# Seven half-size products in the second MLP stage of the first chunk of an attention and MLP kernel

## Chip, cores and metric

The kernel runs on one core of one Trainium2 chip. The metric is the device time of one execution in microseconds (us), the median over runs. All times of instructions come from one profiled execution and are counted from the start of its span.

## What is computed

Linear attention over 8 batches, 8 heads, 576 tokens and head size 64, and behind it a layer norm and an MLP with a residual, in float32 at the edges:

```python
q_s = softmax(q, axis=-1)                      # over the head's 64 numbers
k_s = softmax(k, axis=2)                       # over the tokens
kv = einsum('bhsd,bhse->bhde', k_s, v)
x  = einsum('bhsd,bhde->bhse', q_s, kv)        # heads put side by side: 8 x 576 x 512
xn = (x - mean(x)) / sqrt(var(x) + 1e-06) * g_ln
out = x + maximum(xn @ w_ch1, 0.0) @ w_ch2     # 512 -> 2048 -> 512
```

## The kernel before

**Tiling.** A chunk is 512 tokens of one batch, as four token tiles of 128. Chunks 0 to 7 are the first 512 tokens of batches 0 to 7, and a ninth chunk holds the last 64 tokens of all eight. Work runs chunk by chunk. A chunk has a first MLP stage (16 row tiles of 128 hidden units, from 512 inputs, then relu into hT) and a second stage (16 row tiles of hT as the contraction, 512 output columns). The weights stay in SBUF in bf16: w1_sb (raw), w1g (scaled by g_ln), w2_sb.

**Products.** From chunk 1 on, both stages use a scheme of seven block products in place of eight (for 2 x 2 blocks). It needs sums of blocks ahead of the products: sum_h (line 576) builds four sums of hT blocks on VectorE, quarter_w2 (line 563) four of w2 in w2_q, sum_x (line 255) four of the normed input on GpSimd, and sum_w1 (line 242) four of w1 in the columns of w1_sb whose raw values are no longer needed. Some results are then passed between PSUM banks by a ScalarE copy (copy_u, line 628, and the seeds) and a VectorE add (add_u, line 632). sum_w1 has two parts: part 1 serves the upper eight row tiles, which chunk 1 uses, and part 0 the lower eight, which chunk 2 uses first. In chunk 0 all of the second stage is plain: mm2_stream (line 552) makes 64 matmuls of 512 columns, 16 for each of four token tiles, each tile in its own PSUM bank, and y_out (line 533) takes a bank out by one VectorE instruction of 512 columns and a store.

**Order of the work.** The order on every engine is written out by hand. run (line 849) walks over the matmul steps of a chunk, each with a weight (1 is a matmul of 512 columns, 0.5 one of 256), and issues a side step as soon as the sum of the weights reaches the position given with it. Engines, and the DMA queues of GpSimd and SyncE, then execute what they were given in this order; an instruction that waits holds all behind it on its engine. In chunk 0 the first stage has positions 0 to 64 and the second 64 to 128. Lines 1109 to 1141 are chunk 0's side steps, second_side (line 896) is chunk 1's. Chunk 0's side steps include the preparation of chunk 1: exp_qt and reduce_q (softmax of q), eq_pT (four transposes on TensorE and a ScalarE copy), exp_k and prep_kvrem (exponentials of k), cast_v (copies of v to vm), kv_pairs (line 357: 40 small matmuls, then a reciprocal and two multiplications on VectorE into kv_sb), po_x (line 1104: four matmuls that need kv_sb, then x_fast on VectorE), xn_pT (transposes of the normed chunk).

**Loads.** load_behind (line 1067) puts loads for batches 1 and 2 into the GpSimd queue at the start; its load_krem is the load of the last 64 tokens of k (tile ktr, two DMAs of 64 KB), which prep_kvrem reads. load_batch (line 1077) puts later loads of q and k into the SyncE queue.

Of the kernel before, what the change touches and what calls it, by code (L numbers as in the profile page):

```python
# [12 lines left out]
FP32 = mybir.dt.float32  # L13
BF16 = mybir.dt.bfloat16
AF = mybir.ActivationFunctionType
ALU = mybir.AluOpType
# [4 lines left out]
def kernel(  # L21
# [21 lines left out]
    P = 128  # L43
# [183 lines left out]
    def reduce_q(c, t, tn=1):  # L227
        ts = slice(t, t + tn)
        nc.vector.reduce_sum(eqs[c][1][:, ts], eqs[c][0][:, ts], axis=AX.X)  # L229
# [9 lines left out]
        at = DH // 2 * (1 - part)  # L239
        return w1_sb[:, n, at : at + DH // 2].rearrange("p (ko i n) -> p ko i n", ko=2, n=P)  # L240

    def sum_w1(i, part):

        ps = slice(4 * part, 4 * part + 4)
        blocks = w1g.rearrange("p (kh ko) (i odd n) -> p kh ko i odd n", kh=2, odd=2, n=P)
        a11, a12, a21, a22 = [blocks[:, kh, :, ps, odd, :] for odd in range(2) for kh in range(2)]
        s1, s2, s3, s4 = [w1_sum(n, part) for n in range(4)]
        dst, x, y, op = (
            (s1, a21, a22, ALU.add), (s2, s1, a11, ALU.subtract),
            (s4, a12, s2, ALU.subtract), (s3, a11, a21, ALU.subtract),  # L250
        )[i]
        for ko in range(2):
            nc.vector.tensor_tensor(out=dst[:, ko], in0=x[:, ko], in1=y[:, ko], op=op)

    def sum_x(c, i, ts=range(2)):

# [273 lines left out]
            else:  # L530
                nc.scalar.activation(dst, ph, AF.Relu)

    def y_out(c, t, pc, cols=slice(0, 512), eng=None):
        if cols.start == 0:
            hbox["ot"] = outp.tile([P, DM], FP32, tag="ot", name="ot")
        ot = hbox["ot"][:, cols]
        nc.vector.scalar_tensor_tensor(
            ot, in0=pc, scalar=rstds[c][:, t : t + 1], in1=xs[c][0][:, t, cols],
            op0=ALU.mult, op1=ALU.add,
        )  # L540
        eng = eng or nc.gpsimd
        if c < B:
            eng.dma_start(
                out[c, 0:SM, :].rearrange("(p t) n -> p t n", t=T)[:, t, cols], ot
            )
        else:
            for half in range(2):
                eng.dma_start(
                    out[2 * t + half, SM:S, cols], ot[64 * half : 64 * half + 64]
                )  # L550

    def mm2_stream(c, t, ko):

        if ko == 0:
            hbox["pc", t] = mm_ps.tile([P, DM], FP32, tag="m", name="pc")
        nc.tensor.matmul(  # L556
            hbox["pc", t], hbox["h"][:, ko, t, :], w2_sb[:, ko, :],
            start=(ko == 0), stop=(ko == KO2 - 1),
        )
        if ko == KO2 - 1:  # L560
            y_out(c, t, hbox["pc", t], eng=nc.sync if t > 1 else nc.gpsimd)

    def quarter_w2(i, k0, kn):

        ks = slice(k0, k0 + kn)
# [20 lines left out]
        )[i]  # L586
        nc.vector.tensor_tensor(out=dst, in0=x, in1=y, op=op)  # L587

    def prod(n, bank, t, k, first=False, own=False, c0=0, cn=DH2):

        at = slice(t * P, t * P + P)
        cs = slice(c0, c0 + cn)
        if n in (1, 2, 4):
            odd, half = ((0, 0), (1, 0), None, (1, 1))[n - 1]
            lhsT = hbox["h"][:, 2 * k + odd, 2 * half + t, :]
        else:
            lhsT = hbox["s"][:, {5: 0, 6: 1, 7: 2, 3: 3}[n], k, at]
# [6 lines left out]
        nc.tensor.matmul(hbox[bank][:, t, cs], lhsT, rhs[:, cs],  # L604
                         start=first and (own or t == 0) and k == 0,
                         stop=k == KH - 1, skip_group_check=True)
# [4 lines left out]
    def y_quarter(c, t, col, src):  # L611
        if (c, t) not in ybox:
            ybox[c, t] = outp.tile([P, DM], FP32, tag="ot", name="ot")
            ynum[c, t] = 0
        cols = slice(DH2 * col, DH2 * col + DH2)
        nc.vector.scalar_tensor_tensor(
            ybox[c, t][:, cols], in0=src, scalar=rstds[c][:, t : t + 1],
            in1=xs[c][0][:, t, cols], op0=ALU.mult, op1=ALU.add,
        )
        ynum[c, t] += 1  # L620
        if ynum[c, t] == 2:
            nc.gpsimd.dma_start(
                out[c, 0:SM, :].rearrange("(p t) n -> p t n", t=T)[:, t], ybox[c, t]
            )

# [5 lines left out]

    def add_u(dst, src):
        nc.vector.tensor_tensor(out=hbox[dst], in0=hbox["b"], in1=hbox[src], op=ALU.add)

    def last_products(product):

# [183 lines left out]
    def mlp_steps(c):  # L820
        if c > FAST:
            return mm1_fast(c) + mm2_fast(c)
        first = []
        if c == 0:
            first = [
                (0.5, lambda m=m, ko=ko: mm1_part(c, m, 0, 2, ko))
                for kh in range(2) for m in range(4) for ko in (2 * kh, 2 * kh + 1)
            ]
            parts = ((0, 2, 1), (1, 0, 2), (0, 3, 1), (2, 0, 2), (1, 2, 2), (2, 2, 2), (3, 0, 2), (3, 2, 2))
        else:  # L830
            parts = ((0, 0, 2), (1, 0, 2), (0, 2, 2), (1, 2, 2))
        for n, t0, tn in parts:
            first += [
                (0.25 * tn, lambda m=m, t0=t0, tn=tn, ko=ko: mm1_part(c, m, t0, tn, ko))
                for m in range(4 * n, 4 * n + 4) for ko in range(KO1)
            ]
        if c == 0:
            return first + [
                (1, lambda t=t, ko=ko: mm2_stream(c, t, ko))
                for k0, kn in ((0, 4), (4, 4), (8, 4), (12, 2), (14, 2))  # L840
                for t in range(T) for ko in range(k0, k0 + kn)
            ]
        return first + mm1_fast(c, (2,)) + mm2_fast(c)

    def spread(fns, a, b):
# [50 lines left out]
    def second_side():  # L896
# [6 lines left out]
        s += [(p, lambda j=j: cast_v(2, j)) for j, p in enumerate((23, 32.2))]  # L903
        s += [(at, lambda i=i: sum_x(1, i)) for i, at in enumerate((9.1, 9.2, 31.5, 36))]
        s += [(66, lambda: load_v(3, True))]
        s += [(9 + 2 * t, lambda t=t: reduce_q(2, t, 2)) for t in (0, 2)]
        s += [(36, lambda: recip_q(2))]
        s += [(18, lambda: exp_k(2, 0, 4)), (28.5, lambda: exp_k(2, 2, 4)), (33, lambda: prep_kvrem(2))]
# [158 lines left out]
    def load_behind(b, parts=(2, 0, 1)):  # L1067

        alloc(b, parts)
        for which in parts:  # L1070
            if which == 1:
                load_v(b)
                load_krem(nc.gpsimd, b)
            else:
                load_main(nc.gpsimd, b, which, 0, H)

    def load_batch(b, parts=(2, 0), after=None):

        alloc(b, parts)
        for which in parts:  # L1080
            if after is None:
                nc.vector.memset(raws[b][which][0:1, 0, 0, 0:1], 0.0)
            else:
                nc.gpsimd.tensor_copy(out=raws[b][which][0:1, 0, 0, 0:4], in_=after)
        for which in parts:
            hn = H // 2 if (b, which) == (B - 1, 2) else H
            for h0 in range(0, H, hn):
                load_main(nc.sync, b, which, h0, hn)
        if 0 in parts:
            load_krem(nc.sync, b)  # L1090

    with tc.manual_schedule(
# [2 lines left out]
    ):  # L1095
        first_batch()
        load_behind(1, (2, 0))
        load_w2(2)
        load_behind(1, (1,))
        load_w2(3, 0, 2)  # L1100
        load_w2(3, 2, 2)
        load_behind(2)

        def po_x(c, t):
            for i in range(NP):
# [34 lines left out]
            + [(p, lambda t=t: xn_pT(1, t, nc.scalar)) for t, p in enumerate((119, 122.5, 127.9))]  # L1140
            + [(p + 0.1, lambda t=t: square_sum(1, t)) for t, p in enumerate((119, 122.5))]

        )
        for c in range(1, B):
# [46 lines left out]
```

## Time and profile before

| | |
|---|---|
| median of 3 runs | 262.92 us (262.43 to 263.71) |
| the profiled execution's own time | 262.68 us |
| its span | 260.9 us |
| TensorE (PE) busy, granted clock | 254.9 us (98%), 0.997 |
| VectorE (DVE), ScalarE (ACT), GpSimd (POOL) busy | 223.3, 177.8, 103.4 us |
| chunk 0, first stage | about 15.2 to 31.3 us |
| chunk 0, second stage | 31.3 to 48.6 us |
| chunk 1 | 48.6 to 76.2 us |

The span runs from the first to the last instruction; 1.78 us of the execution's own time lie outside it. A line of the timeline gives the start, the time from the first start to the last end of the merged instructions, engine, source line, operation, tiles, shapes and count, and in brackets how long the engine was idle before it and what ended that. Since an instruction's end overlaps the start of the next on its engine, the step from one start to the next is shorter than a duration.

### The profile page before, as it was taken

Reading aid. Unit: us, or ns where it says so; the run is one execution under the profiler, and the core shown is the slowest. Engines: PE = TensorE matmul, PEld = TensorE weight load, DVE = VectorE, ACT = ScalarE, POOL = GpSimd, SP = SyncE. Lnnn points to the kernel's source line nnn. Section 1 sums busy time; section 2 is a strip of 40 time slices with the busy share of each in tenths; the row PEclk is TensorE's granted clock in tenths of the full one; section 3 lists DMA queues with packets and bytes.
Section 4 is the critical chain, followed back from the end, with each engine's and each line's share of the span. In section 5 each row is a group of like instructions: output and inputs, shape, how many; then the busy total and the mean of one; then the engine's idle time right before and its main releaser. Section 6 shows DMA issues by size and latency. Waiting matters only on the chain.

```text
span 260.9 us, 7328 instructions
## 1 busy us (share of the span) xinstructions
PE 254.9 (98%) x2904; PEld 218.6 (84%) x2907; DVE 223.3 (86%) x542; ACT 177.8 (68%) x348; POOL 103.4 (40%) x160
## 2 busy tenths in 40 slices
PE   8999999999999999999999999999999999999993
PEld 5889855788888888888888888888888888888883
DVE  6778996989998998899889988998899889957873
ACT  4657790997987785788578857885788386638400
POOL 3953138230199409800890098009100910190000
PEclk9999999999999999999999999999999999999998
DMA  6999999998899996998889968998902630322014
GB/s 190 255 206 206 352 221 274 275 213 273 151 121 314 272 110 139 293 242 88 119 287 259 95 133 290 244 96 166 276 1 45 140 143 4 72 72 101 3 40 121
DMA packets 82618, 45.04 MB, mean 173 GB/s; under 512 B 58196, under 2 KB 79192, under 8 KB 82584
## 3 DMA queue, kind: packets, MB, share of 16 engines
q0 software_dynamic: 32464, 21.76, 44.9%
q1 hardware_dynamic: 49488, 22.29, 37.0%
q10 hardware_dynamic: 632, 0.53, 0.7%
q8 instruction: 22, 0.36, 0.6%
q14 instruction: 12, 0.10, 0.1%
HBM read 36.70 MB, written 9.44 MB: 177 GB/s over the span
## 4 chain that ended last, share of the span: by engine, by line
PE 92%; DMA 4%; POOL 2%; issue 0%; DVE 0%
PE ba L604 21%; PE bx L762 20%; PE bb L762 10%; PE ph L520 8%; PE bb L604 6%; PE be L604 5%; PE bc L604 5%; PE pc L556 5%; PE bc L762 5%; DMA w_raw<-in_moe_w_ch_dram 3%; PE pkv L371 2%; DMA qt<-in_q_dram 2%; PE po L403 2%; PE ptr L928 1%; PE po L414 1%; POOL v L1006 1%
## 5 line engine op out<-in xcount | busy, mean ns | idle before, releaser
L604 PEld LDWEIGHTS <-hs 128*128 128x128 bf16 x512 | 49.6, 98 | 6.0
L269 POOL TENSOR_TENSOR tq<-xnT 128x256 bf16<-128x256 bf16 x30 | 20.1, 671 | 85.5 <-PE bc L604 59.9
L762 PEld LDWEIGHTS <-w_raw 128*128 128x128 bf16 x480 | 46.6, 98 | 5.8 <-DVE bb L793 0.2
L604 PEld LDWEIGHTS <-hT 128*128 128x128 bf16 x392 | 37.6, 98 | 4.2
L762 PEld LDWEIGHTS <-w1g 128*128 128x128 bf16 x360 | 34.7, 98 | 4.3 <-issue 0.2
L762 PE MATMUL bx<-tq,w_raw 128*128 128x256 bf16 x240 | 31.5, 273 | 0.0
L604 PE MATMUL ba<-w_q,hs 128*128 128x256 bf16 x256 | 30.6, 273 | 0.0
L786 ACT COPY bc<-bx 128x512 f32<-128x512 f32 x30 | 16.7, 594 | 19.1 <-PE bx L762 19.1
L427 ACT ACTIVATE scrap<-x,mv 128x512 bf16<-128x512 bf16 x32 | 23.1, 723 | 4.6 <-DVE mv L457 4.4
L793 DVE TENSOR_TENSOR bb<-bx,s 128x512 f32<-128x512 f32 x30 | 19.5, 694 | 7.8 <-ACT s L790 5.1
L804 ACT ACTIVATE hT<-bb 128x512 bf16<-128x512 f32 x30 | 16.3, 594 | 9.5 <-PE bb L762 9.5
L804 ACT ACTIVATE hT<-bc 128x512 bf16<-128x512 f32 x30 | 16.4, 595 | 8.5 <-PE bc L762 8.5
L796 DVE TENSOR_TENSOR hT<-bx,s 128x512 bf16<-128x512 f32 x30 | 19.3, 684 | 2.9 <-PE bx L762 2.7
L587 DVE TENSOR_TENSOR hs<-hT 128x1024 bf16<-128x1024 bf16 x32 | 21.3, 672 | 0.5 <-ACT hT L804 0.5
L229 DVE TENSOR_REDUCE zq<-eq 128x16 f32<-128x1024 bf16 (+1 forms) x20 | 20.7, 1048 | 0.5 <-ACT eq L220 0.5
L269 POOL TENSOR_TENSOR tq<-xnT,tq 128x256 bf16<-128x256 bf16 x30 | 20.0, 669 | 1.1
L449 DVE SCALAR_TENSOR_TENSOR x<-po,rq 128x256 bf16<-128x256 f32 x48 | 17.5, 420 | 1.6 <-PE po L403 1.6
L790 ACT COPY s<-bb 128x512 f32<-128x512 f32 x30 | 16.5, 620 | 0.0
L804 ACT ACTIVATE hT<-bx 128x512 bf16<-128x512 f32 x30 | 16.4, 608 | 0.0
L762 PE MATMUL bx<-xnT,w1g 128*128 128x256 bf16 x120 | 16.2, 273 | 0.0
L762 PE MATMUL bx<-tq,w1g 128*128 128x256 bf16 x120 | 15.9, 272 | 0.0
L762 PE MATMUL bc<-xnT,w1g 128*128 128x256 bf16 x120 | 15.8, 273 | 0.0
(157 smaller groups left out, 539.3 us busy)
## 6 DMA issues: line engine op xcount, KB each, us to landing
out_dram<-ot POOLq DMA_DIRECT2D x30, 256.0 KB, 5.0
kt<-in_k_dram SPq DMA_DIRECT2D x5, 1024.0 KB, 12.5
qt<-in_q_dram SPq DMA_DIRECT2D x4, 1024.0 KB, 8.7
qt<-in_q_dram POOLq DMA_DIRECT2D x2, 1024.0 KB, 12.9
kt<-in_k_dram POOLq DMA_DIRECT2D x2, 1024.0 KB, 14.7
vm<-in_v_dram POOLq DMA_DIRECT2D x16, 128.0 KB, 12.5
qt<-in_q_dram SPq DMA_DIRECT2D x3, 512.0 KB, 7.2
w_raw<-in_moe_w_ch_dram POOLq DMA_DIRECT2D x3, 512.0 KB, 10.8
```

The costliest lines, as they stand in the source:

```text
L229: nc.vector.reduce_sum(eqs[c][1][:, ts], eqs[c][0][:, ts], axis=AX.X)
L269: nc.gpsimd.tensor_tensor(out=dst[:, t], in0=x[:, t], in1=y[:, t], op=ALU.subtract)
L427: nc.scalar.activation(scrap, x[:, t], AF.Square, bias=mv[:, t, 0:1], scale=-float(DM), accum_out=mv[:, t, 1:2],)
L449: nc.vector.scalar_tensor_tensor(x[:, t].rearrange("p (i two d) -> p i two d", two=2, d=D)[:, :, half], in0=pobox[c, t][half], scalar=1.0, ...
L520: nc.tensor.matmul(ph[:, m % 2, at : at + tn], (w1g if c else w1_sb)[:, ko, m * P : (m + 1) * P], xnTs[c][:, t0 : t0 + tn, ko, :], start=( ...
L587: nc.vector.tensor_tensor(out=dst, in0=x, in1=y, op=op)
L604: nc.tensor.matmul(hbox[bank][:, t, cs], lhsT, rhs[:, cs], start=first and (own or t == 0) and k == 0, stop=k == KH - 1, skip_group_check= ...
L762: nc.tensor.matmul(dst[:, q], lhsT, rhs, start=first and q == 0 and ko == 0, stop=ko == 1, skip_group_check=True)
L786: nc.scalar.copy(at[g, "c"], at[g, "x"])
L793: nc.vector.tensor_tensor(out=at[g, "b"], in0=at[g, "x"], in1=at[g, "s"], op=ALU.add)
L796: nc.vector.tensor_tensor(out=h_out(g, 1, 1), in0=at[g, "x"], in1=at[g, "s"], op=ALU.add)
L804: nc.scalar.activation(h_out(g, odd, half), at[g, name], AF.Relu)
```

## The change

Chunk 0's second stage is split by the contraction. For hT's row tiles 0 to 7 (paired even and odd, four pairs) seven products of eight matmuls with 256 columns replace 32 matmuls with 512. Row tiles 8 to 15 stay plain, as 64 matmuls of 256 columns that add into the same four banks. The second stage has 60 units of weight after, in place of 64, and the side steps at its end are placed four units lower. The four sums of hT (sum_h0) go on VectorE into four buffers of the output pool, at positions 44 to 52. There sum_w1 for part 1 stood; it moves to positions 81 to 89. sum_w1 for part 0, which stood at 66 to 84, moves to GpSimd in chunk 1, at positions 40 to 55. Results leave by y_quarter in eight pieces of 256 columns. The last tokens of k for batch 1 are loaded from SyncE's queue at position 26 and no longer from GpSimd's. SyncE's loads of k for batch 4, and of q and k for batches 5 to 7, are each issued in two halves.

```diff
-    def sum_w1(i, part):
+    def sum_w1(i, part, eng=nc.vector):
...
-            nc.vector.tensor_tensor(out=dst[:, ko], in0=x[:, ko], in1=y[:, ko], op=op)
+            eng.tensor_tensor(out=dst[:, ko], in0=x[:, ko], in1=y[:, ko], op=op)
...
+    def sum_h0(i):
+        if i == 0:
+            hbox["s0"] = [
+                outp.tile([P, KH // 2, 2 * P], BF16, tag="ot", name="s0") for _ in range(4)
+            ]
...
+        dst, x, y, op = (
+            (s1, a21, a22, ALU.add), (s2, s1, a11, ALU.subtract),
+            (s3, a11, a21, ALU.subtract), (s4, a12, s2, ALU.subtract),
+        )[i]
+        nc.vector.tensor_tensor(out=dst, in0=x, in1=y, op=op)
...
-            nc.gpsimd.dma_start(
+            (nc.sync if c == 0 and t > 1 else nc.gpsimd).dma_start(
                 out[c, 0:SM, :].rearrange("(p t) n -> p t n", t=T)[:, t], ybox[c, t]
             )
...
+    def mm2_first():
...
+        product(1, "a", True, {7: [seed_c]})
+        product(5, "b", True)
+        product(6, "a", False, {7: [lambda: copy_u("s2")]})
+        product(2, "c", False, {1: [seed_e]})
+        product(7, "a", False, {7: [lambda: copy_u("s3")]})
+        product(3, "e", False, {1: [lambda: add_u("b", "s3")]})
+        product(4, "a")
+        for k0, kn in ((8, 4), (12, 2), (14, 2)):
+            for name, half, col in (("c", 0, 0), ("e", 0, 1), ("b", 1, 1), ("a", 1, 0)):
+                rest(name, half, col, k0, kn)
+        return steps
...
-            return first + [
-                (1, lambda t=t, ko=ko: mm2_stream(c, t, ko))
-                for k0, kn in ((0, 4), (4, 4), (8, 4), (12, 2), (14, 2))
-                for t in range(T) for ko in range(k0, k0 + kn)
-            ]
+            return first + mm2_first()
...
+        s += [(40 + 5 * i, lambda i=i: sum_w1(i, 0, nc.gpsimd)) for i in range(4)]
...
-                load_krem(nc.gpsimd, b)
+                if b > 1:
+                    load_krem(nc.gpsimd, b)
...
-            hn = H // 2 if (b, which) == (B - 1, 2) else H
+            hn = H // 2 if b > 4 or (b, which) == (4, 0) else H
...
+        nc.vector.memset(raws[1][3][0:1, 0, 0:1], 0.0)
...
+        def krem_first():
+            nc.vector.memset(raws[1][3][0:1, 0, 0:1], 0.0)
+            load_krem(nc.sync, 1)
...
-            + [(62 + t, lambda t=t: exp_qt(1, t)) for t in range(T)]
-            + [(67 + t, lambda t=t: reduce_q(1, t)) for t in range(T)]
-            + [((75, 79, 86, 90)[t], lambda t=t: eq_pT(1, t, nc.scalar)) for t in range(T)]
-            + [(78, lambda: nc.vector.reciprocal(eqs[1][2], eqs[1][1]))]
-            + [(82, lambda: exp_k(1, 0, 4)), (88, lambda: exp_k(1, 2, 4))]
+            + [((68.6, 69.6, 77.1, 78.1)[t], lambda t=t: exp_qt(1, t)) for t in range(T)]
+            + [((78, 79, 84.6, 86)[t], lambda t=t: reduce_q(1, t)) for t in range(T)]
+            + [((76, 79.5, 86, 90)[t], lambda t=t: eq_pT(1, t, nc.scalar)) for t in range(T)]
+            + [(92, lambda: nc.vector.reciprocal(eqs[1][2], eqs[1][1]))]
+            + [(86.5, lambda: exp_k(1, 0, 4)), (90.5, lambda: exp_k(1, 2, 4))]
...
-            + [(p, lambda i=i: quarter_w2(i, 0, 4)) for i, p in enumerate((58, 60, 61, 62))]
-            + [(98.5 + 0.4 * j, lambda j=j: cast_v(1, j)) for j in range(2)]
-            + [(p, lambda i=i: sum_w1(i % 4, 1 - i // 4)) for i, p in enumerate((42, 45, 50, 53, 66, 70, 80, 84))]
-            + [(99 + i, lambda i=i: quarter_w2(i, 4, 2)) for i in range(4)]
-            + [(100.4, lambda: prep_kvrem(1))]
-            + [(110, lambda: (kv_pairs(1), start_x(1)))]
-            + [(p, lambda t=t: po_x(1, t)) for t, p in enumerate((114.8, 116.5, 118.6, 121))]
+            + [(p, lambda i=i: sum_h0(i)) for i, p in enumerate((44, 46, 49.5, 52))]
+            + [(p, lambda i=i: quarter_w2(i, 0, 4)) for i, p in enumerate((56, 57, 58, 59))]
+            + [(p, lambda i=i: sum_w1(i, 1)) for i, p in enumerate((81, 83, 87, 89))]
+            + [(26, krem_first)]
+            + [(p, lambda j=j: cast_v(1, j)) for j, p in enumerate((94.5, 98.5))]
+            + [(98.6 + i / 10, lambda i=i: quarter_w2(i, 4, 2)) for i in range(4)]
+            + [(92, lambda: prep_kvrem(1))]
+            + [(106, lambda: (kv_pairs(1), start_x(1)))]
+            + [(p, lambda t=t: po_x(1, t)) for t, p in enumerate((110.8, 112.5, 114.6, 117))]
```

rest(name, half, col, k0, kn) adds the matmuls of row tiles k0 to k0 + kn - 1 for two token tiles and 256 columns into a bank, and behind the last of them calls y_quarter. seed_c copies bank a into bank c on ScalarE; seed_e adds bank b and s2 into bank e on VectorE.

More of the change, by code (lines that the diff above doesn't have):

```diff
@@ L531, in mm1_part @@
                 nc.scalar.activation(dst, ph, AF.Relu)
[L533 to L561, printed above, removed]
     def quarter_w2(i, k0, kn):
@@ L587, in sum_h, with h_sum, prod @@
         nc.vector.tensor_tensor(out=dst, in0=x, in1=y, op=op)
-    def prod(n, bank, t, k, first=False, own=False, c0=0, cn=DH2):
+    def sum_h0(i):
[3 more added lines that the diff above has]
+            ]
+        s1, s2, s3, s4 = hbox["s0"]
+        a11, a12, a21, a22 = [
+            h_part(odd, half, slice(0, KH // 2)) for half in range(2) for odd in range(2)
+        ]
+        dst, x, y, op = (
[3 more added lines that the diff above has]
+        nc.vector.tensor_tensor(out=dst, in0=x, in1=y, op=op)
+    def h_sum(n, k, at, c):
+        i = {5: 0, 6: 1, 7: 2, 3: 3}[n]
+        return hbox["s0"][i][:, k, at] if c == 0 else hbox["s"][:, i, k, at]
+    def prod(n, bank, t, k, first=False, own=False, c0=0, cn=DH2, c=None):
         at = slice(t * P, t * P + P)
@@ L596, in prod @@
         else:
-            lhsT = hbox["s"][:, {5: 0, 6: 1, 7: 2, 3: 3}[n], k, at]
+            lhsT = h_sum(n, k, at, c)
         if n in (1, 2):
@@ L633, in add_u, with product, go, rest @@
         nc.vector.tensor_tensor(out=hbox[dst], in0=hbox["b"], in1=hbox[src], op=ALU.add)
+    def mm2_first():
+        steps = []
+        def product(n, name, first=False, at=None):
+            for i in range(KH):
+                t, k = divmod(i, KH // 2)
+                def go(t=t, k=k, i=i):
+                    if first and i == 0:
+                        bank(name)
+                    prod(n, name, t, k, first, c=0)
+                    for fn in (at or {}).get(i, []):
+                        fn()
+                steps.append((0.5, go))
+        def rest(name, half, col, k0, kn):
+            for t in range(2):
+                for ko in range(k0, k0 + kn):
+                    def go(t=t, ko=ko):
+                        nc.tensor.matmul(
+                            hbox[name][:, t], hbox["h"][:, ko, 2 * half + t, :],
+                            w2_sb[:, ko, DH2 * col : DH2 * col + DH2],
+                            start=False, stop=ko == KO2 - 1, skip_group_check=True,
+                        )
+                        if ko == KO2 - 1:
+                            y_quarter(0, 2 * half + t, col, hbox[name][:, t])
+                    steps.append((0.5, go))
+        def seed_c():
+            bank("c")
+            nc.scalar.copy(hbox["c"], hbox["a"])
+        def seed_e():
+            bank("e")
+            add_u("e", "s2")
+        product(1, "a", True, {7: [seed_c]})
[9 more added lines that the diff above has]
+        return steps
     def last_products(product):
@@ L1140 @@
-            + [(p, lambda t=t: xn_pT(1, t, nc.scalar)) for t, p in enumerate((119, 122.5, 127.9))]
-            + [(p + 0.1, lambda t=t: square_sum(1, t)) for t, p in enumerate((119, 122.5))]
+            + [((68.6, 69.6, 77.1, 78.1)[t], lambda t=t: exp_qt(1, t)) for t in range(T)]
+            + [((78, 79, 84.6, 86)[t], lambda t=t: reduce_q(1, t)) for t in range(T)]
+            + [((76, 79.5, 86, 90)[t], lambda t=t: eq_pT(1, t, nc.scalar)) for t in range(T)]
+            + [(92, lambda: nc.vector.reciprocal(eqs[1][2], eqs[1][1]))]
@@ L1143 @@
+            + [(98.6 + i / 10, lambda i=i: quarter_w2(i, 4, 2)) for i in range(4)]
+            + [(92, lambda: prep_kvrem(1))]
+            + [(106, lambda: (kv_pairs(1), start_x(1)))]
+            + [(p, lambda t=t: po_x(1, t)) for t, p in enumerate((110.8, 112.5, 114.6, 117))]
+            + [(p, lambda t=t: xn_pT(1, t, nc.scalar)) for t, p in enumerate((115, 118.5, 123.9))]
+            + [(p + 0.1, lambda t=t: square_sum(1, t)) for t, p in enumerate((115, 118.5))]
         )
```

## The prediction

> **What bounds the kernel.** First the page's busy times, then the chain of waits, then TensorE's timeline.
>
> ```profile
> PE 254.9 (98%) x2904; PEld 218.6 (84%) x2907; DVE 223.3 (86%) x542; ACT 177.8 (68%) x348; POOL 103.4 (40%) x160
> PE   8999999999999999999999999999999999999993
> ```
>
> TensorE is busy from the second slice to the last but one, and the chain gives it 92%. So time falls only where TensorE has less to do, and rises where it is made to wait. The stage that changes:
>
> ```profile
> 34.99 1.67 PE L556 MATMUL pc<-w_sb,hT 128*128 128x512 bf16 x7
> 36.50 0.39 PE L928 MATMUL ptr<-ident,eq 128*128 128x128 bf16 x4
> 43.21 1.03 PE L556 MATMUL pc<-w_sb,hT 128*128 128x512 bf16 x4 [0.16 <-issue]
> 44.22 0.38 PE L414 MATMUL po<-kv_sb,eqT 128*128 128x128 bf16 x4
> ...
> 65.60 1.91 PE L604 MATMUL bb<-w_q,hs 128*128 128x256 bf16 x16
> 67.35 1.91 PE L604 MATMUL ba<-w_q,hs 128*128 128x256 bf16 x16
> ```
>
> A matmul of 512 columns takes (36.50 - 34.99) / 7 = 0.2155 us, one of 256 takes (67.35 - 65.60) / 16 = 0.1091. The stage lasts from 31.31 to 48.63. Its 64 matmuls are 13.79 us, seven transpose groups 7 x 0.22, four po groups 4 x 0.22, kv_pairs 0.76: 16.97, and so only 0.35 is waiting. VectorE is the second engine, and its end of this stage is what po waits for:
>
> ```profile
> 33.45 0.75 DVE L253 TENSOR_TENSOR w_raw<-w1g 128x512 bf16<-128x512 bf16 x2
> 34.12 2.46 DVE L229 TENSOR_REDUCE zq<-eq 128x8 f32<-128x512 bf16 x4
> ...
> 41.30 0.87 DVE L570 TENSOR_TENSOR w_q<-w_sb,w_q 128x512 bf16<-128x512 bf16 x2
> 43.09 0.18 DVE L377 RECIPROCAL rzk<-pkv 128x4 f32<-128x4 f32 x1 [0.92 <-PE pkv L371]
> 43.31 0.86 DVE L379 TENSOR_TENSOR kv_sb<-pkv,rzk 64x256 bf16<-64x256 f32 x2
> 44.64 0.69 DVE L464 SCALAR_TENSOR_TENSOR x<-po,rq 128x512 bf16<-128x512 f32 x1 [0.47 <-PE po L414]
> ```
>
> VectorE had 0.92 us to spare ahead of rzk; kv_sb is ready at 43.31 + 0.86 = 44.17, and po starts at 44.22.
>
> **TensorE's own work.** 64 x 0.2155 = 13.79 becomes 56 x 0.1091 + 64 x 0.1091 = 13.09: 0.70 less. The loads of weights double, but a load takes 98 ns and lies under 109 ns, as in every later chunk.
>
> **Bank a is handed on three times.** Products 1, 6, 7 and 4 all write it, and between two of them lie eight matmuls, 0.87 us, where later chunks have sixteen. A ScalarE copy must fit in.
>
> ```profile
> 65.80 0.57 ACT L714 COPY bc<-ba 128x512 f32<-128x512 f32 x1 [0.16 <-PE ba L604]
> ```
>
> It starts 0.20 behind the issue of the last matmul (65.60) and takes 0.57; with 0.05 to get back that is 0.82 of 0.87. Where ScalarE is free it costs nothing: seed_c runs from 32.38 to 32.95, the next product wants the bank at 33.06. For s2, two exp_qt (0.53 each) are over just as product 6 ends, and two transpose groups widen the gap: nothing. For s3, ScalarE is at eq_pT's copy until 36.64: the copy ends at 37.23, bank a was wanted at 37.20: 0.09. The three copies (0.48 of ScalarE's time each) stand in a stretch where it is busy for 6.67 of 11.0 us.
>
> **VectorE's queue, step by step.** The step from one instruction to the next is: sum of 128x1024, 0.60; sum_w1 pair, 0.67; reduce_q, 0.59; add_u, 0.61 (72.52 - 71.91); cast, 0.33; the last four quarter_w2, 1.46; the first four, 2.53. At 27.04 VectorE is free as before, but sum_h0 needs the relu of row tiles 4 and 5, which ScalarE ends at 27.10 + 0.61. Two sums to 28.96, relu 29.56, two sums 30.77, quarters 33.30, relu 33.90. (t1 is there at 31.4, product 5 wants it at 32.18.) Next in the queue is now seed_e, and it waits for the s2 copy: product 6 ends at 31.31 + 24 x 0.1091 = 33.93, the copy at 34.13 + 0.59 = 34.72, seed_e starts at 34.77. Behind it stand two reduce_q, two sum_w1, add_u, two reduce_q, two sum_w1, the reciprocal, the casts and the quarters, all needed ahead of rzk: 0.61 + 1.18 + 1.34 + 0.61 + 1.18 + 1.34 + 0.26 + 0.66 + 1.46 = 8.64, so VectorE reaches rzk at 43.41, against 43.09. The 2.7 us of sum_w1 part 0 that it loses are spent on two adds (1.22), on sums that come in place of others, and on two waits (0.7 and 0.9).
>
> TensorE is at kv_pairs at 31.31 + 6.11 + 0.88 + 0.09 + 28 x 0.1091 = 41.44; it waits 0.3 there for the casts, and is at po at about 43.6. kv_sb is ready at 43.41 + 0.22 + 0.86 = 44.49 and po starts at 44.54, 0.32 later than before, after a wait of some 0.9. From po to the stage's end are 26 half-size matmuls in place of 13 (+0.04). So the stage ends 0.36 later: **the 0.70 is not seen, because VectorE becomes the bound at po**. A late VectorE could also hold banks: it takes y out in eight steps of 0.40 in place of four of 0.68, 0.5 more, and ends near 52.2 against 51.35; bank c is free at 49.8 where chunk 1 asks for it at 49.8 to 50.3, so 0 to 0.3, taken as 0.
>
> **The moved sums on GpSimd.** Eight instructions of 128x512. The nearest row is L269 (128x256, 0.67, step 0.63); bounds are 0.67 if a fixed cost rules and 1.26 if it goes by size. I take 1.25 as sum_x goes by data: 10 us. They start behind the cast at 58.38, here near 58.8, and end at 69.
>
> ```profile
> 58.38 0.18 POOL L1084 CAST qt<-eqT 1x4 f32<-1x4 bf16 x1 [4.29 <-DMA eqT<-eq]
> 70.59 1.56 POOL L161 DMA_DIRECT2D vt<-in_v_dram  x2 [12.04 <-DVE hs L587]
> ```
>
> GpSimd waits in this gap anyway, so up to 11.8 us are hidden. What is queued behind are the loads vt and vr and sum_x of chunk 2, whose t1 ends at 76.80 where product 5 asks for it at 77.02: past the cover every us costs one. Against VectorE there is a question, the second rival.
>
> **The smaller moves.** ktr leaves GpSimd's queue (issues at 30.02 and 32.60), so the last two w2 loads start some 5 us earlier; they were on time. On SyncE it waits for a memset on VectorE (0.06) near 23, and nothing but the stores at 50.72 stands behind it. It lands near 33.5 by the page's 10.5 us; before, ScalarE waited until 41.71 for it, and that 0.17 of TensorE's waiting goes, but the casts are late next. kt of batch 2 still waits for exp_k (near 40.3, issue at 40.62 before). The halved loads serve chunks in which TensorE does not wait (each lasts about 26.1 us): 0, and a late one could cost up to the 0.4 of an issue. Sum: 262.68 + 0.36 = 263.0, against the execution's own time, which is 0.24 under the median of 262.92.
>
> **Rivals.** (1) *VectorE keeps up.* If its queue is 0.9 us shorter than I add up, po goes by TensorE: kv_pairs at 41.44, rzk 0.87 later as before, kv_sb 1.08 later, po at 43.44: 0.78 - 0.04 = 0.74 saved, **261.9**. For: my steps come from a stretch with few gaps, and two 0.33 steps are uncertain. Against: the queue is strictly in order, and each of these instructions is there.
>
> (2) *GpSimd's sums hold up VectorE in chunk 1* (slower). In the trace VectorE's instructions of one kind take longer when GpSimd is at work:
>
> ```profile
> 132.10 3.86 POOL L166 DMA_DIRECT2D vm<-in_v_dram  x4
> ...
> 135.03 0.86 DVE L801 TENSOR_SCALAR hT<-hT 128x1024 bf16<-128x1024 bf16 x1
> 141.37 0.43 DVE L801 TENSOR_SCALAR hT<-hT 128x1024 bf16<-128x1024 bf16 x1
> ```
>
> 0.86 against 0.43 without GpSimd. In the before trace GpSimd's sums never run beside VectorE's sums of two SBUF tensors (L587); after, they would, from 62.4 to 69. If each excludes the other for a whole instruction, taking turns: L801 waits until 63.65, xn until 65.2, the first hs sum until 66.65, xn until 68.45, the second hs sum until 69.9. Product 5 wants the first at 65.95 and the second 0.87 behind it: waits of 1.35 and 2.35, together 3.7, **266.7**; with half of the turns lost, 264.9. It decides from 0.42 us of delay on: that is the room of the second sum before (ready 66.05, wanted 66.47). For: L801. Against: L269 stays at 0.67 beside other VectorE work.
>
> [...]
>
> (3) *GpSimd too late for chunk 2.* If its sums take 1.7 each they end at 72.4, 1.8 behind the 70.59, and chunk 2 waits 1.6: **264.6**. L269's spread (0.66 to 0.73) speaks against it.
>
> **How the numbers follow.** Forecast 0.46 (262.6 to 263.9), rival 1 0.24 (261.4 to 262.6; a fifth of it below 261.6), rival 2 0.24 (264.2 to 266.7), rival 3 0.04, the rest (banks, an unlucky queue) 0.02. The range 261.8 to 265.8 leaves out the lower end of rival 1 and the upper half of rival 2. 0.5% is 1.3 us, about what a measurement of this kernel can tell from no change. Faster by more than that needs the whole 0.70, the 0.35 of waiting and more: 0.05. Slower: rivals 2, 3 and rest, 0.30 less a little: 0.28. Within: 0.67.
>
> **What would show it.** Right: TensorE waits 0.7 to 1 us ahead of po with VectorE's kv_sb as releaser, rzk near 43.4 without idle time in front, chunk 1's first matmul near 49.0; L587 in chunk 1 at 0.68 and no new wait of L604 for it. Wrong: rzk waiting for pkv (rival 1); L801 or L587 longer, or started late, between 62 and 70, with products 5 and 6 of chunk 1 waiting for hs (rival 2); product 5 of chunk 2 waiting for tq (rival 3); matmuls of 256 columns at more than 0.109.

## The result, and the profile after

The changed kernel takes **273.55 us** (median of 4, 272.56 to 274.73) beside 263.31 for the kernel before in the same comparison (262.43 to 263.71): a ratio of **1.0395**, interval 1.0335 to 1.0456. The forecast was 263.0 with a range to 265.8; it was wrong by 10.5 us, and "slower", to which it gave 0.28, is what came.

The profiled execution took 274.73, 1.2 over the median, with a span of 272.9. Two rows and the chain's shares from its page:

```profile
PE 258.9 (95%) x2963; PEld 226.5 (83%) x2963; DVE 227.7 (83%) x546; ACT 179.6 (66%) x351; POOL 111.4 (41%) x166
PEclk9999999979799999999999999999999999999999
PE 81%; DVE 10%; DMA 4%; POOL 1%; issue 1%; ACT 0%; ACTq 0%; DVEq 0%
```

TensorE's share fell from 98% to 95%, although its records add up to *more* busy time than before (258.9 against 254.9) for less work: the clock row has sevens in slices 9 and 11, where matmuls last longer (behind 55.39, in slice 9, 12 of them take 2.77 in place of 1.47). VectorE has taken a tenth of the chain that ended last. Both point at a stretch near 50 to 80 us. TensorE's start times at fixed places of its order say where each microsecond arises:

| place in TensorE's order | before | after | difference | of it new |
|---|---|---|---|---|
| first matmul of the first MLP stage | 15.24 | 16.58 | 1.34 | +1.34 (a load, see the runs) |
| second stage of chunk 0 | 31.31 | 32.73 | 1.42 | +0.08 |
| kv_pairs | 42.22 | 43.11 | 0.89 | -0.53 |
| first po | 44.22 | 46.20 | 1.98 | +1.09 |
| first matmul of chunk 1 | 48.63 | 55.39 | 6.76 | **+4.78** |
| chunk 1, products of the first stage | 55.84 | 63.93 | 8.09 | **+1.33** |
| chunk 1, first po | 59.98 | 69.95 | 9.97 | **+1.88** |
| chunk 1, second stage | 63.63 | 75.56 | 11.93 | **+1.96** |
| chunk 2 | 76.15 | 88.01 | 11.86 | -0.07 |

So all of it arises before 76 us, most between po of chunk 0 and the second stage of chunk 1. The stage that was to be shorter is shorter up to kv_pairs, by 0.53; what follows takes it back twenty times.

**The last 6 us of chunk 0's stage.** TensorE's timeline there (start, length, engine, line, operation, and in brackets the idle time before it and its releaser):

```profile
48.44 0.39 PE L414 MATMUL po<-kv_sb,eqT 128*128 128x128 bf16 x4
50.15 0.38 PE L647 MATMUL bc<-w_sb,hT 128*128 128x256 bf16 x2 [1.32 <-DVE ot L606]
...
51.93 0.38 PE L647 MATMUL be<-w_sb,hT 128*128 128x256 bf16 x2 [0.96 <-DVE ot L606]
...
53.28 0.38 PE L647 MATMUL bb<-w_sb,hT 128*128 128x256 bf16 x2 [0.75 <-DVE ot L606]
...
54.62 0.55 PE L647 MATMUL ba<-w_sb,hT 128*128 128x256 bf16 x2 [0.75 <-DVE ot L606]
```

In the kernel before, each bank held one token tile, and VectorE read the four banks behind all matmuls of the stage:

```profile
48.63 2.72 DVE L537 SCALAR_TENSOR_TENSOR ot<-pc,rstd,x 128x512 f32<-128x512 f32 x4
```

Now each bank holds two token tiles side by side. In the diff's `rest`, y_quarter for the first token tile stands directly behind that tile's last matmul, so the second tile's two matmuls *into the same bank* come behind VectorE's read of the first half. VectorE's side in the changed kernel, from 49.23 on:

```profile
49.23 0.08 DVE L464 DVE_READ_ACCUMULATOR x<-po,rq 128x1 f32 x1
49.35 0.35 DVE L439 TENSOR_SCALAR xn<-x,mv 128x512 bf16<-128x512 bf16 x1
49.62 0.48 DVE L606 SCALAR_TENSOR_TENSOR ot<-bc,rstd,x 128x256 f32<-128x256 f32 x1
```

The read of bank c's first half ends at 49.62 + 0.48 = 50.10, and TensorE goes on at 50.15. It stood in VectorE's queue behind x and xn of the residual path, which take 0.68, 0.08 and 0.35 for every token tile; the read of the second half, after another such three, starts at 51.01, and the reads of be, bb and ba queue behind that. The four waits are 1.32 + 0.96 + 0.75 + 0.75 = **3.78 us**. The matmuls write other columns than VectorE reads, and yet each of the four waits ends 0.05 or 0.06 behind VectorE's read of the *other* half: the reads end at 50.10, 51.87, 53.23 and 54.56, and TensorE goes on at 50.15, 51.93, 53.28 and 54.62. The prediction did not weigh a wait between the two halves of one bank.

**The slow matmuls behind it.** Two stretches of the span. The columns are the length, then busy time and count of TensorE, its weight loads, VectorE, ScalarE and GpSimd, then the granted clock, the DMA share and GB/s:

```profile
50.00:55.00 5.00, 2.39 (x19) 1.66 (x19) 3.59 (x10) 1.30 (x3) 1.13 (x2) 0.97 0.73 171
55.00:58.00 3.00, 3.00 (x18) 2.26 (x17) 1.19 (x2) 2.23 (x4) 0.67 (x1) 0.50 0.45 175
```

TensorE was at work for 2.39 of 5 us, and then got half its clock for about 3 us. The first 12 matmuls of chunk 1, before and then after:

```profile
48.63 1.47 PE L520 MATMUL ph<-xnT,w1g 128*128 128x256 bf16 x12
```

```profile
55.39 2.77 PE L520 MATMUL ph<-xnT,w1g 128*128 128x256 bf16 x12
```

So the first stage of chunk 1 lasts 63.93 - 55.39 = 8.54 in place of 55.84 - 48.63 = 7.21.

**VectorE and GpSimd in chunk 1.** Three of VectorE's instructions there in the kernel before; the same three after (L570 is now L540); then GpSimd after:

```profile
56.67 0.42 DVE L146 COPY vm<-vt 128x1024 bf16<-128x1024 bf16 x1
57.00 0.41 DVE L570 TENSOR_TENSOR w_q<-w_sb,w_q 128x512 bf16<-128x512 bf16 x1
57.34 0.41 DVE L266 TENSOR_TENSOR tq<-xnT,tq 128x512 bf16<-128x512 bf16 x1
```

```profile
64.74 1.31 DVE L146 COPY vm<-vt 128x1024 bf16<-128x1024 bf16 x1
65.97 1.37 DVE L540 TENSOR_TENSOR w_q<-w_sb,w_q 128x512 bf16<-128x512 bf16 x1
67.26 1.37 DVE L266 TENSOR_TENSOR tq<-xnT,tq 128x512 bf16<-128x512 bf16 x1
```

```profile
64.62 2.44 POOL L253 TENSOR_TENSOR w_raw<-w1g 128x512 bf16<-128x512 bf16 x2
67.02 2.62 POOL L253 TENSOR_TENSOR w_raw<-w_raw,w1g 128x512 bf16<-128x512 bf16 x2
```

From the moment that GpSimd's sums run, L146, L540 and L266 each last 1.3 to 1.4, about as long as one sum, where the same forms took 0.42: here the two engines take turns, one instruction each. The first three sums end at 65.76, 67.05 and 68.35, L146, L540 and L266 at 66.05, 67.34 and 68.63, each 0.28 or 0.29 behind one sum. Some 2.8 us of VectorE's time go. The kv_sb that chunk 1 prepares for chunk 2 is late, and the first po that needs it waits:

```profile
69.95 0.22 PE L414 MATMUL po<-kv_sb,eqT 128*128 128x128 bf16 x1 [1.70 <-DVE kv_sb L379]
```

Behind that wait the clock falls again (0.50 in 72 to 74), and the way from po to the second stage is 1.96 longer, of which 0.19 is a wait for VectorE's add (bb, L835).

### The profile page after: what moved, and what is told of

Read it like the earlier page. It is cut to its first block, busy times and chain, and to the rows that moved or that the text cites. A ratio compares the mean times of both kernels' runs of the same rounds, so it can differ in the third digit from the quotient of the medians.

```text
span 272.9 us, 7474 instructions
## 1 busy us (share of the span) xinstructions
PE 258.9 (95%) x2963; PEld 226.5 (83%) x2963; DVE 227.7 (83%) x546; ACT 179.6 (66%) x351; POOL 111.4 (41%) x166
## 4 chain that ended last, share of the span: by engine, by line
PE 81%; DVE 10%; DMA 4%; POOL 1%; issue 1%; ACT 0%; ACTq 0%; DVEq 0%
PE ba L594 20%; PE bx L804 19%; PE bb L804 10%; PE ph L520 8%; PE be L594 5%; PE bb L594 5%; PE bc L804 5%; PE bc L594 4%; DMA w_raw<-in_moe_w_ch_dram 3%; DMA qt<-in_q_dram 1%; PE po L403 1%; PE pkv L371 1%; DVE ot L606 1%; DVE w_q L540 1%; DVE w_raw L253 1%; DVE x L464 1%
## 5 line engine op out<-in xcount | busy, mean ns | idle before, releaser
L269 POOL TENSOR_TENSOR tq<-xnT 128x256 bf16<-128x256 bf16 x30 | 20.1, 668 | 90.1 <-PE bc L594 41.8
L594 PEld LDWEIGHTS <-hT 128*128 128x128 bf16 x416 | 39.9, 98 | 4.5
L835 DVE TENSOR_TENSOR bb<-bx,s 128x512 f32<-128x512 f32 x30 | 19.5, 694 | 7.8 <-ACT s L832 5.2
L846 ACT ACTIVATE hT<-bc 128x512 bf16<-128x512 f32 x30 | 16.5, 595 | 10.2 <-PE bc L804 10.2
L557 DVE TENSOR_TENSOR hs<-hT 128x1024 bf16<-128x1024 bf16 x32 | 21.3, 672 | 0.5 <-ACT hT L846 0.5
L269 POOL TENSOR_TENSOR tq<-xnT,tq 128x256 bf16<-128x256 bf16 x30 | 20.0, 668 | 1.1
L612 POOL DMA_DIRECT2D out_dram<-ot x30 | 16.6, 559 | 5.9 <-DVE ot L606 5.9
L620 ACT COPY s<-ba 128x512 f32<-128x512 f32 x17 | 10.0, 587 | 10.6 <-DVE hs L557 5.8
L804 PE MATMUL bb<-xnT,w_raw 128*128 128x256 bf16 x120 | 16.6, 282 | 0.0
L804 PE MATMUL bx<-tq,w1g 128*128 128x256 bf16 x120 | 16.6, 279 | 0.0
```

Of the source, the lines that this page charges most:

```text
L269: nc.gpsimd.tensor_tensor(out=dst[:, t], in0=x[:, t], in1=y[:, t], op=ALU.subtract)
L594: nc.tensor.matmul(hbox[bank][:, t, cs], lhsT, rhs[:, cs], start=first and (own or t == 0) and k == 0, stop=k == KH - 1, skip_group_check= ...
L612: (nc.sync if c == 0 and t > 1 else nc.gpsimd).dma_start(out[c, 0:SM, :].rearrange("(p t) n -> p t n", t=T)[:, t], ybox[c, t])
L804: nc.tensor.matmul(dst[:, q], lhsT, rhs, start=first and q == 0 and ko == 0, stop=ko == 1, skip_group_check=True)
L835: nc.vector.tensor_tensor(out=at[g, "b"], in0=at[g, "x"], in1=at[g, "s"], op=ALU.add)
L846: nc.scalar.activation(h_out(g, odd, half), at[g, name], AF.Relu)
```

## The experiments

Four causes could hold: the bank halves, the sums on GpSimd, VectorE's longer queue ahead of the first po, and the loads (a w_raw load was 1.34 late in the profiled execution). The runs were to put a price on each. Times are medians, and "excess" is the median less that of the kernel before on the same chip. The ratios' intervals are about 1.5 us wide to either side for the changed kernel and e2, and about 0.7 for e3, so a difference of two excesses is known to 1.5 or 2 us.

### e1: both token tiles taken out behind the bank's last matmul

```diff
-                        if ko == KO2 - 1:
-                            y_quarter(0, 2 * half + t, col, hbox[name][:, t])
+                        if ko == KO2 - 1 and t == 1:
+                            for i in range(2):
+                                y_quarter(0, 2 * half + i, col, hbox[name][:, i])
```

> Changed kernel, but a bank's two pieces of y are both taken out behind the last matmul of its second token tile. Theory bank (the second tile's matmuls wait for VectorE's read of the first tile's half of the same bank): the four waits of 1.32, 0.96, 0.75 and 0.75 us go, and the slow-clock stretch behind them (1.3): 273.5 - 5.1 = 268.4. Theory backlog (VectorE is simply late in chunk 0, and the waits only show it): the waits come back at chunk 1's banks, 272 or more. Theory sums (GpSimd's sums cost 3.4 in chunk 1) says nothing of this run.

Measured: 272.74, 264.49, 274.87 and 273.50 (median 273.1, excess 10.1; before 263.0). The waits on the banks are gone, as they had to be, and yet three executions of four are no faster. The number is that of the backlog theory, but its sign is missing: no wait stands at chunk 1's banks. TensorE's longest wait is now elsewhere; VectorE's and GpSimd's timelines show why:

```profile
57.65 9.28 DVE L266 TENSOR_TENSOR tq<-xnT,tq 128x512 bf16<-128x512 bf16 x1
```

```profile
57.74 2.26 POOL L253 TENSOR_TENSOR w_raw<-w1g 128x512 bf16<-128x512 bf16 x2
...
64.40 2.25 POOL L253 TENSOR_TENSOR w_raw<-w1g 128x512 bf16<-128x512 bf16 x2
```

```profile
68.25 0.26 PE L414 MATMUL po<-kv_sb,eqT 128*128 128x128 bf16 x1 [7.77 <-DVE kv_sb L379]
```

An instruction of 0.42 us takes 9.28: it starts as GpSimd's eight sums begin and ends 0.28 after their last (64.40 + 2.25 = 66.65). Here the engines do not take turns; VectorE is kept out for the whole run of sums. kv_sb waits behind it in VectorE's queue, TensorE for kv_sb: 7.77.

### e2: the change without the sums on GpSimd

```diff
-        s += [(40 + 5 * i, lambda i=i: sum_w1(i, 0, nc.gpsimd)) for i in range(4)]
```

> Changed kernel without the four sums of w1 for chunk 2 (left out, so chunks 2 and later use raw w1 columns in their place). Theory sums (they hold up VectorE's casts, tq sums and quarter_w2 by some 2.8 us, kv_pairs of chunk 2 comes late and the clock falls): L146, L540 and L266 near 62 to 69 back at 0.42, po's wait of 1.70 and the second slow-clock stretch (1.5) gone: 273.5 - 3.4 = 270.1. Theory bank alone, or theory backlog: 273.5, as the lateness comes from chunk 0.

Measured: 269.53 (267.53 to 270.50), ratio 1.0245 (1.0193 to 1.0298), excess 6.5. The four bank waits are there again (1.3, 1.0, 0.6, 0.6), and L146, L540 and L266 are back at 0.42; the last of them:

```profile
64.82 0.42 DVE L266 TENSOR_TENSOR tq<-xnT,tq 128x512 bf16<-128x512 bf16 x1
```

So the sums cost the changed kernel 10.2 - 6.5 = 3.7, and what is left is not theirs.

### e3: both edits

> Both edits: y behind the pair, and the four sums of w1 for chunk 2 left out. If bank and sums are the two causes and add up: 273.5 - 5.1 - 3.4 = 265.0, or 263.1 to 263.6 if the late first load in the profiled run (1.4) was that run's own. Theory backlog: above 268.

Measured: 263.59 (262.95 to 265.17), ratio 1.0034 (1.0009 to 1.0059), excess 0.6. TensorE at the first po and at chunk 1, and VectorE ahead of it:

```profile
44.91 0.38 PE L414 MATMUL po<-kv_sb,eqT 128*128 128x128 bf16 x4 [0.73 <-DVE kv_sb L379]
...
49.34 0.82 PE L520 MATMUL ph<-xnT,w1g 128*128 128x256 bf16 x6
```

```profile
43.79 0.17 DVE L377 RECIPROCAL rzk<-pkv 128x4 f32<-128x4 f32 x1
```

This is the timeline that was forecast: rzk follows without idle time, po waits for kv_sb, and the stage, from 31.44 to 49.34, is 17.90 where it was 17.32 before. The price of the bank halves is e2 less e3: 6.5 - 0.6 = **5.9**. With the first-half reads in place, the sums cost 3.7; with those gone (e1 less e3) **9.5** in three executions of four. So the two causes are not additive. The bank waits shift VectorE against GpSimd: as the sums begin, VectorE is at L146 in the changed kernel and already at L266 in e1. That this shift is what makes the difference is not shown.

### e4: the sums alone, in the kernel before

```diff
-            + [(p, lambda i=i: sum_w1(i % 4, 1 - i // 4)) for i, p in enumerate((42, 45, 50, 53, 66, 70, 80, 84))]
+            + [(p, lambda i=i: sum_w1(i, 1)) for i, p in enumerate((42, 45, 50, 53))]
...
+        s += [(40 + 5 * i, lambda i=i: sum_w1(i, 0, nc.gpsimd)) for i in range(4)]
```

> Kernel before with one part of the change alone: sum_w1 part 0 leaves VectorE in chunk 0 and goes to GpSimd in chunk 1 at positions 40 to 55. Theory sums: GpSimd's sums run from 58.6 to 69 and hold up L801, xn and the hs sums as the second rival put it, 263.3 + 1.4 to + 4 = 264.7 to 267.3. Theory bank alone or backlog: 263.3 or a little under, since VectorE has 2.7 us less to do in chunk 0.

Measured: 268.35 (267.91 to 269.19), ratio 1.0220 (1.0188 to 1.0251), excess 5.4: above the range given. VectorE, then TensorE behind it:

```profile
61.91 4.55 DVE L801 TENSOR_SCALAR hT<-hT 128x1024 bf16<-128x1024 bf16 x1
```

```profile
68.11 3.55 PE L604 MATMUL bb<-w_q,hs 128*128 128x256 bf16 x16 [2.86 <-DVE hs L587]
```

The second rival's place, L801 and hs, with a larger size: L801 is held to the end of GpSimd's last sum (66.16), not for one of them. Then the 16 matmuls last 3.55 in place of 1.91, at a clock of 0.57 (68 to 72).

### e5 and e6: what does the hold last for?

e5 is e1 with each sum on GpSimd cut in two, 16 of 128x256. e6 is e3 with the first pair of sums alone on GpSimd (`range(1)` in place of `range(4)`); the other three are left out.

> e1 with GpSimd's eight sums of 128x512 cut into sixteen of 128x256 (about 0.63 each). Theory turn (VectorE's instruction waits for the GpSimd instruction that runs, then they alternate): no wait of VectorE over 0.7 us; VectorE loses some 4 x 0.6 ahead of kv_sb, 264.5 to 266 in every run. Theory run (GpSimd's instructions behind one another keep VectorE out until the last is done): one VectorE instruction of 9 to 10 us as in e1, 272 to 275 in most runs.

> e3 with only the first of the four sums on GpSimd (two instructions, 2.25 us; the other three are left out, so chunks 2 and later use wrong columns there). Theory run: a VectorE instruction is held up to 2.25 us near 58, kv_sb of chunk 2 comes up to 1.7 late: 264 to 265.5. Theory turn: held 1.1 at most, and 0.5 of that is idle time: 263.6 to 264.2. If the sums cost by being there at all and not by time held: as e1, 270 or more.

Measured: e5 275.13, 273.95, 266.85 and 273.00 (median 273.5); e6 265.17 (264.31 to 265.98), ratio 1.0088 (1.0059 to 1.0116). VectorE and GpSimd in e5, then in e6:

```profile
58.76 10.42 DVE L270 TENSOR_TENSOR tq<-xnT,tq 128x512 bf16<-128x512 bf16 x1
```

```profile
58.85 2.54 POOL L255 TENSOR_TENSOR w_raw<-w1g 128x256 bf16<-128x256 bf16 x4
...
66.36 2.54 POOL L255 TENSOR_TENSOR w_raw<-w1g 128x256 bf16<-128x256 bf16 x4
```

```profile
57.37 2.64 DVE L266 TENSOR_TENSOR tq<-xnT,tq 128x512 bf16<-128x512 bf16 x1
```

```profile
57.46 2.26 POOL L253 TENSOR_TENSOR w_raw<-w1g 128x512 bf16<-128x512 bf16 x2
```

Smaller pieces do not let VectorE in (10.42, to 69.18; the last piece ends at 68.90). Two sums hold it for 2.64. In e1, e5 and e6 the hold goes with the length of the unbroken run on GpSimd: 9.28 beside 8.91 (57.74 to 66.65), 10.42 beside 10.05 (58.85 to 68.90) and 2.64 beside 2.26. In e6 po then waits 1.13, and the granted clock shows no drop behind it (the wait lies in slice 10 of 40):

```profile
61.32 0.22 PE L414 MATMUL po<-kv_sb,eqT 128*128 128x128 bf16 x1 [1.13 <-DVE kv_sb L379]
```

```profile
PEclk9999999999999999999999999999999999999998
```

### e11 and e12: the changed kernel and e1 looked at again

> The changed kernel, a second look. Theory bank: the four waits of bc, be, bb and ba for ot again, about 3.8 us together. Theory run: whether VectorE alternates with GpSimd's sums (three instructions of 1.3 us, po's wait 1.7) or is kept out to the end of the sums (one of up to 9 us) can go either way; 272.6 to 274.7 if it alternates.

> e1, a second look: it gave 264.5 once and 273 to 275 three times. Theory run: near 273, one VectorE instruction of about 9 us; near 264.5, none of them over 1.5 us.

Measured: e11 272.66, e12 273.59. e11 takes turns once more (L146 1.28, L540 1.38, L266 1.37; bank waits 1.32, 0.96, 0.75 and 0.75), e12 is shut out once more (L266 9.27, po waits 7.8). So the pattern belongs to the kernel, in both profiled executions of each. But the single times of 264.49 in e1 and 266.85 in e5 were not profiled; that these had the other pattern is likely and not shown.

### e7: the loads alone, in the kernel before

The diff's krem on SyncE and the halved loads, and nothing else.

> Kernel before with the moves of loads alone: k's last tokens for batch 1 from SyncE's queue at position 26, and the halved loads of k for batch 4 and of q and k for batches 5 to 7. All theories: 263.2, no difference; if the loads take part in the 10 us, 264.5 or more.

Measured: 263.19 (262.53 to 264.57), ratio 1.0006 (0.9976 to 1.0036): no difference. And TensorE's wait for its first loads is 0.16 in the profile of before, 1.48 in that of after, 0.44 in e3 and none in e2, whose order of loads is that of after. The changed kernel's second profile (e11) has 0.34. It varies from execution to execution and is not the change's.

### e8: e3 with VectorE's idle time filled

VectorE waits for the s2 copy and for the relu in the new stage. One sum goes into each gap, so that fewer stand ahead of rzk.

```diff
-            + [(p, lambda i=i: sum_w1(i, 1)) for i, p in enumerate((81, 83, 87, 89))]
+            + [(p, lambda i=i: sum_w1(i, 1)) for i, p in enumerate((43, 70, 83, 87))]
```

> e3 (sums for chunk 2 left out, y behind the pair) with two of VectorE's sum_w1 part 1 moved into its idle times, positions 43 and 70 in place of 81 and 83. The forecast's step for chunk 0 (VectorE, late by 0.7 to 0.9 us, is the bound at po): rzk comes 1.3 us earlier, po's wait of 0.73 and kv_pairs' of 0.2 go, 263.6 - 0.8 = 262.8. If TensorE's work or bank handing is the bound there: 263.6.

Measured: 262.66 (262.15 to 264.62), ratio 0.9994 (0.9971 to 1.0017). The stage lasts from 30.78 to 47.91, 17.13 in place of e3's 17.90, and po's wait is shorter (0.73 in e3):

```profile
43.47 0.38 PE L414 MATMUL po<-kv_sb,eqT 128*128 128x128 bf16 x4 [0.47 <-DVE kv_sb L379]
```

So it was VectorE's queue that held the saving of TensorE. Even then, with four sums left out, the kernel is level with the one before.

### e9 and e10: the sums on GpSimd held back to where VectorE lets them be free

The sums must be done somewhere. In e9, made from the kernel before, the last two sums go to GpSimd, each behind a one-element memset by VectorE that fixes where it may start. e10 is a whole kernel: e8, with two of the missing sums on VectorE in chunk 0 and two on GpSimd behind such memsets, and all stores of chunk 0 by SyncE.

```diff
+    def sum_w1_behind(i):
+        nc.vector.memset(w1_sum((0, 1, 3, 2)[i], 0)[0:1, 0, 0, 0:1], 0.0)
+        sum_w1(i, 0, nc.gpsimd)
...
+            + [(89 + i, lambda i=i: sum_w1(i, 0)) for i in range(2)]
+            + [(117.05, lambda: sum_w1_behind(3))]
...
+        s += [(40.5, lambda: sum_w1_behind(2))]
```

> Kernel before with the last two sums of part 0 on GpSimd, each held back by a one-element memset on VectorE to a stretch in which VectorE has no instruction with two SBUF inputs or a fast SBUF copy: behind chunk 1's last x_fast (48.7 to 51) and behind kv_sb of chunk 2 (59.7 to 62). Theory hold (by turn or by run; only those VectorE instructions are kept out): no VectorE instruction longer than 0.75, 263.0 (262.8 to 263.4). If any GpSimd sum slows VectorE: 264 or more.

> The changed kernel made complete without its two faults: y behind the pair, VectorE's idle times filled as in e8, the first two sums of part 0 on VectorE in chunk 0 (1.3 us), the last two on GpSimd, held back to stretches without shared VectorE work (behind chunk 1's last x_fast, and behind kv_sb of chunk 2), all stores of chunk 0 from SyncE. Theory hold and theory backlog: VectorE is at rzk 1.3 us later than in e8, so 262.7 + 0.9 = 263.6, no gain over the kernel before. If VectorE has room there: 262.7.

Measured: e9 264.25 (263.03 to 266.34), ratio 1.0048 (1.0020 to 1.0077); e10 264.80 (263.63 to 265.96), ratio 1.0063 (1.0038 to 1.0087). Both missed the theories' 263.0 and 263.6, by 1.2 each; e9 came in the case set at 264 or more, a GpSimd sum that slows VectorE. e9's GpSimd, then VectorE:

```profile
52.20 0.57 POOL L547 DMA_DIRECT2D out_dram<-ot  x1 [6.02 <-DVE w_raw L256]
52.79 2.28 POOL L253 TENSOR_TENSOR w_raw<-w1g,w_raw 128x512 bf16<-128x512 bf16 x2
...
55.60 1.31 POOL L273 TENSOR_TENSOR tq<-xnT 128x256 bf16<-128x256 bf16 x2
```

```profile
56.66 2.11 DVE L574 TENSOR_TENSOR w_q<-w_sb 128x512 bf16<-128x512 bf16 x2
```

The moved sum held nothing up, but it came late, and what it pushed back did: GpSimd's sum_x ran into L574, 2.11 where such a pair takes 0.75. That is TensorE's wait of 0.9 for hT there; the 1.6 that the same execution waited for its first loads is the varying wait of e7. In e10, with the stores out of the way, no VectorE instruction beside the two pairs (49.33 and 60.32, 2.27 and 2.26) is longer than elsewhere (L610 0.87 and L840 1.30 a pair, L616 0.88 and L793 1.30 in the kernel before). Its excess is 8.5 us smaller than the changed kernel's, and it is still not below the one before: the two sums on VectorE put rzk back to 43.55 and the stage to 17.90, e3's length. About 1 us of its excess of 1.7 is not accounted for.

## Why the prediction was wrong, and where it was right

**Wrong: "a late VectorE could also hold banks … so 0 to 0.3, taken as 0".** This is the largest failure: a term put at 0 that measured 3.78 us of waits in the profile, 5.9 with what follows (e2 less e3). The step looked for a bank asked for by chunk 1, and worked out when the *last* read ends. It never asked what stands between the two token tiles of *one* bank. The diff shows it: `rest` loops over t outside ko and calls y_quarter inside. In the kernel before, a bank held one token tile, and nothing was written to it behind its read. The rows priced both halves of the wait: y_quarter's 0.40, and the x and xn (0.68 + 0.08 + 0.35) that it queues behind. Bank c's 1.32 is about those.

**Wrong: "GpSimd waits in this gap anyway, so up to 11.8 us are hidden".** GpSimd's time was hidden, and its size was near (1.14 to 1.33 a sum, forecast 1.25), but VectorE's was not. The second rival had this with 0.24. That the two engines exclude each other for a whole instruction was its assumption, which the trace of before does not show; the changed kernel shows L146, L540 and L266 at 1.31, 1.37 and 1.37 in place of 0.42, and L557 (L587 before), where the rival put them, at 0.68, since GpSimd's run was over by then (74.27). Its size by turns, 3.7, is also what the sums cost the changed kernel (10.2 - 6.5), but that is luck, as the place is another: the turns fall on the cast, the quarter and tq ahead of kv_sb, and po of chunk 1 waits, not products 5 and 6. The forecast let the sums begin 58.8 - 49.0 = 9.8 us behind chunk 1's first matmul, behind tq; they began after 64.62 - 55.39 = 9.23 in the changed kernel, whose VectorE was late, and after 57.74 - 48.94 = 8.80 in e1. And turns are only one of two patterns. In e1, e4, e5, e6 and e12 VectorE is kept out to the end of GpSimd's run, at 1.2 for two sums (e6 less e3), 5.4 (e4) and 9.5 (e1 less e3). L146 and L540 of the changed kernel are held for one sum (1.31 and 1.37), L266 in e1 for eight (9.28 beside a run of 8.91). What decides between the two patterns stays open. It is not the form of the instruction, as L266 is held in e1 (9.28) and takes turns in the changed kernel (1.37). It is not the order of the starts alone either: the held L266 of e1 starts 0.09 before the first sum, the held L801 of e4 0.22 behind the start of a pair of sums (61.69). The evidence that the prediction weighed was not of this case: L801's 0.86 was an instruction with one SBUF input beside DMA issues of GpSimd, and L269's 0.67 "beside other VectorE work" was taken as a sign against; in e9 a pair of L574 took 2.11 in place of 0.75 beside the same sum_x (there L273).

**Not priced: the clock.** Both waits were paid for a second time, about 1.3 us behind the bank waits and up to 1.8 behind po of chunk 1. The prediction read the granted clock nowhere, since it reads 9 in every slice of before but the last.

**Right: "the 0.70 is not seen, because VectorE becomes the bound at po".** With the two causes out, e3 has rzk behind a queue without idle time, po's wait 0.73 (forecast 0.9), the stage 0.58 longer (forecast 0.36), and 1.0034 in time. e8 tests the reason: shorten VectorE's queue and the stage is 0.77 shorter. Matmuls of 256 columns stay at 0.109 ((32.31 - 31.44) / 8 in e3). Handing on bank a was 0.09 by forecast and some 0.05 in e3 (product 4 starts at 37.40 in place of 37.35), though the prediction's row of the copy was misread: the last matmul of ba there is issued at 65.49, and 65.60 is the first of the next bank. In e3 TensorE has done the work ahead of kv_pairs 10.11 us into the stage (forecast 10.13); kv_pairs then starts 0.27 later, 0.05 behind the end of the first cast (41.40 + 0.37), which is why its start moved by 0.53 and not by 0.78.

**Right: the smaller moves at 0** (e7: 1.0006).

Put together, 5.9 for the bank halves, 3.7 for the sums beside them and 0.6 for the stage itself are the 10.2 of the result. They add up by construction, as each is the difference of two runs, and the split goes by the order in which the edits are undone: from e1 on the sums alone would count 9.5.

## What to carry to other kernels

Where a PSUM bank holds several tiles, issue its reads only behind the *last* matmul into that bank, and look in every loop for a read between two writes to one bank: here such reads, behind all that stood in VectorE's queue, made four waits of 3.78 us together. Work moved to an engine with idle time is free only if it does not hold up another engine: keep long runs of GpSimd sums away from stretches where VectorE casts or sums SBUF tensors on the way to TensorE's next wait (instructions of 0.42 took 1.3 to 10.42 beside them). And price a long TensorE wait twice, once for itself and once for the clock behind it: here single waits of 1.70 (the changed kernel), 2.86 (e4) and 7.77 (e1) were followed by a clock of 0.50, 0.57 and 0.50, and four of 1.32 to 0.75 in a row by 0.50, while behind single waits of 0.73 (e3), 1.13 (e6) and 1.48 (the changed kernel's first loads) it showed no fall.

## What the runs showed of the hardware that was not expected

- **Half the clock after half-busy stretches.** The waits in 48 to 55 of the changed kernel are 1.32, 0.96, 0.75 and 0.75, TensorE was at work for 2.39 of the last 5 us, and the granted clock was 0.50 for about 3 us. Four waits, none longer than 1.32, lay ahead of it. In e3, TensorE was at work for 3.27 of the 4 us from 44 to 48, with one wait of 0.73, and the clock stayed at 1.00, as it did behind e6's wait of 1.13.
- **VectorE shut out for a whole run of GpSimd instructions**: 9.28 us beside eight sums, 10.42 beside sixteen half-size ones, 4.55 for what was left of a run of eight (e4), 2.64 beside two (e6); in the changed kernel the same forms took turns at 1.3 each.
- **The first loads' landing varies**: TensorE waits between nothing and 1.6 us for them; in two executions of the changed kernel it waited 1.48 and 0.34.
